# A last chunk of 512 tokens, keys copied in halves, 64 by 64 quarters of the array for eight pairs of heads, and a new list order

## The chip, the cores and the metric

The kernel runs on one core of one Trainium2 chip. The metric is device time in microseconds of one execution; the time before is the median of 3 runs, 616.33 us (616.15 to 616.97). The engines are TensorE (matmuls and transposes, PE in the rows; its weight loads have a row of their own, PEld), VectorE (DVE), ScalarE (ACT), GpSimd (POOL), and SyncE (SP), which issues the DMAs. Each engine works through its own instructions in the order in which the program gives them, and waits at an instruction until its inputs are there and its output may be overwritten.

## The reference

For q, k, v of 2 batches, 8 heads, 768 positions and 64 channels, each query sees the 31 keys less than 16 positions away and 24 block keys, each the maximum over 32 positions of k; the values of the blocks are means of v. Scores are scaled by 1/8, block scores get log(32) added, and a softmax runs over both kinds together. The heads are put side by side to 1536 tokens of 512 channels. Two feed-forward layers of width 2048 follow:

```
x = attention(q, k, v)                                 # 1536 x 512
h = max(x @ w_in1, 0);  x = (h * h) @ w_out1
h = x @ w_in2
g = (a0 + a1 h + a2 h^2 + a3 h^3) / (1 + |b0| |h| + |b1| h^2 + 1e-6)
out = g @ w_out2
```

## The kernel before

**The feed-forward layers.** Each factor is split into a high and a low part (xh and xl, wh and wl, sh and sl), and a product is three matmuls: high by high, high by low, low by high. A layer's 16 slices of 128 hidden channels are split over two passes, 5 and 11 for the first layer (passes 0 and 1), 9 and 7 for the second. A pass goes over chunks of tokens; pass 0 has six of 256 tokens (`tok1`, line 543), the later passes three of 512 (`tok2`). A step is one slice for one chunk: `l1` (line 555) makes its hidden values in four parts of three matmuls each, `elem_1` and `elem_2` the square of the ReLU, `elem_4` and `elem_5` the split, and `l2` (line 641) adds the slice's share to the chunk's output in four parts of three matmuls. The output of a chunk lies in PSUM banks y0 to y3 (two of them for 256 tokens) until its last slice, then it is copied to SBUF (`acc`).

**The attention.** Work is done in 24 duos: two heads with 256 queries each; duos 0 to 3 are the 8 heads at the first 256 tokens, and so on, so that chunk c of pass 0 needs the duos 4c to 4c + 3. The queries of a duo form four windows of 64; a window's keys are 96 positions and 24 blocks, 120 columns. A duo goes through: `d_t` (two transposes of q), `d_z` (copy to SBUF; each head to its own half of the depth, the other half zeros, two copies on ScalarE), `d_s` (scores: a matmul of 128 x 128 by 120 columns for each window, the 128 rows being the two heads' 64 channels), `d_m` (mask and maximum, VectorE), `d_e` (exponential, ScalarE), `d_r` (sum and reciprocal, VectorE), `d_n` (scaling, GpSimd), `d_p` (four transposes), `d_b` (copy to SBUF, ScalarE or VectorE), `d_o` (eight products with the values), `d_x` and `d_y` (the split into xh and xl, ScalarE and VectorE). The matmuls of fp32 operands, as in `d_s` and `d_o`, show two instructions each in the trace.

The keys are loaded for two heads at a time (`e_load`), put into another order by GpSimd (`k_rel`, line 297, one copy a pair), transposed (`k_tr`), and copied into windows (`k_lin`, two halves). `k_put` adds the block maxima. Block sums of v come from `s_add` and `v_sum`, and `v_put` copies them.

**The order.** Pass 0 and the attention are interleaved by a list written out in the program, `ORDER` (line 19): each entry is a letter for a function and a number, and a star puts its copy on VectorE. The letters of the table at line 719 are: E, Q, q_, J loads of k and q; v, Z, N loads of v; I, T, D, W, M load, three conversion steps and the low half of a weight (DMA, ScalarE, VectorE, ScalarE, GpSimd); P the key copy, t, l, k, c, B the rest for the keys; S, V, u, w block sums of v; q, z, s, m, e, r, n, p, b, o, x, y the stages of a duo; h part of an `l1` (four to a step), i, j, G, H the elementwise work of a step, Y a part of an `l2`. Each engine gets its instructions in the order of this list. What follows the list, from the end of pass 0 on, is laid out by `main_loop`, in which TensorE goes from step to step. PSUM banks for the attention come from a small pool (`bank`, `free`), first in first out.

Of the kernel before, what the change touches and what calls it, by code (L numbers as in the profile page):

```python
# [59 lines left out]
def tile_window_attention_moe_moe(  # L60
# [27 lines left out]
    NWIN = S // LO  # L88
    SC = math.sqrt(D)
    NEG = -1e9 * SC  # L90
    NSLOT, NMORE = 10, 3

    const = ctx.enter_context(tc.tile_pool(name="const", bufs=1))
    wp = ctx.enter_context(tc.tile_pool(name="wp", bufs=NSLOT))
# [763 lines left out]
```

## Time and profile before

| | |
|---|---|
| median of 3 runs | 616.33 us |
| the profiled execution: its own time | 617.99 us |
| its span, first to last instruction | 616.3 us |
| TensorE matmuls busy | 597.6 us, 97% |
| TensorE weight loads busy | 514.0 us, 83% |
| VectorE busy | 390.8 us, 63% |
| ScalarE busy | 402.1 us, 65% |
| GpSimd busy | 345.9 us, 56% |
| granted TensorE clock, mean | 0.999 of full speed |
| first matmul of pass 0 (h0) | 33.18 us |

Busy time of matmuls is the union of overlapping records, so it doesn't say how many fit in. Idle time of an engine counts only where TensorE then waits for it. The mean duration in a group of instructions is that of one instruction from start to end; the time that one more of it takes is the distance between starts in a packed row. A list of waits names what came last before the waiting instruction could start.

### The profile page before, as it was taken

The page shows a single profiled execution, that of the slowest core. Times are in us where ns is not written, and L with a number is a line of the kernel's source. Part 1 is how long each engine was busy: PE and PEld are TensorE (multiplying, and loading weights), DVE is VectorE, ACT ScalarE, POOL GpSimd, SP SyncE. Part 2 cuts the span into 40 slices and gives each one's busy share as a digit, 9 for nine tenths or more (in the row PEclk, how much of TensorE's full clock was granted, in tenths as well). Part 3 has the DMA queues.
Part 4 walks back from the last instruction along what each step waited for, and adds up shares of the span by engine and source line. Part 5 has one row for each costly group of instructions (what it writes and reads, how often), then busy time and mean ns, then how long its engine had stood idle before and what let it go on. Part 6 is the DMA issues. An engine that isn't in the chain of part 4 may idle for free.

```text
span 616.3 us, 9787 instructions
## 1 busy us (share of the span) xinstructions
PE 597.6 (97%) x3488; PEld 514.0 (83%) x3488; DVE 390.8 (63%) x815; ACT 402.1 (65%) x766; POOL 345.9 (56%) x363
## 2 busy tenths in 40 slices
PE   5899998999999999999999999999999999999997
PEld 4789898999988888888888888888888888888885
DVE  5998777666553332111256487898878887686775
ACT  5887566766554443222356598988888887777772
POOL 4777858355664445222557568675656664454442
PEclk9999999999999999999999999999999999999999
DMA  9999894440342331000045202121202200010011
GB/s 220 247 225 213 208 233 96 120 108 16 114 160 72 99 103 35 0 1 0 1 137 179 96 1 69 34 70 34 69 35 69 69 1 0 1 69 1 22 47 68
DMA packets 64145, 51.48 MB, mean 84 GB/s; under 512 B 39777, under 2 KB 56161, under 8 KB 64097
## 3 DMA queue, kind: packets, MB, share of 16 engines
q1 hardware_dynamic: 64096, 50.87, 30.8%
q8 instruction: 27, 0.44, 0.3%
q14 instruction: 22, 0.17, 0.1%
HBM read 47.71 MB, written 3.15 MB: 83 GB/s over the span
## 4 chain that ended last, share of the span: by engine, by line
PE 80%; DVE 1%; ACT 0%; POOL 0%; issue 0%; DVEq 0%; ACTq 0%
PE h L567 39%; PE y L661 38%; PE pss L452 1%; PE pav L517 1%; PE ptp L501 1%; DVE acc L687 0%; PE pt L433 0%; DVE h L616 0%; DVE q L613 0%; ACT h L609 0%; POOL wl L175 0%; DVE p L619 0%; ACT q L588 0%; DVE p L602 0%; DVE pp L505 0%
## 5 line engine op out<-in xcount | busy, mean ns | idle before, releaser
L567 PE MATMUL h<-xh,wh 128*128 128x512 f32 (+1 forms) x444 | 161.9, 365 | 0.0
L567 PE MATMUL h<-xh,wl 128*128 128x512 f32 (+1 forms) x444 | 160.1, 361 | 0.0
L567 PE MATMUL h<-xl,wh 128*128 128x512 f32 (+1 forms) x444 | 160.0, 360 | 0.0
L637 POOL TENSOR_TENSOR sl<-r,sh 128x512 fp32r<-128x512 f32 (+1 forms) x63 | 66.4, 1054 | 119.8 <-PE y L661 76.6
L591 POOL TENSOR_TENSOR q<-q,u 128x512 f32<-128x512 f32 x48 | 63.8, 1330 | 94.7 <-ACT q L588 91.0
L582 DVE TENSOR_TENSOR r<-r,h 128x512 f32<-128x512 f32 (+1 forms) x63 | 35.0, 555 | 113.1 <-ACT r L577 105.6
L567 PEld LDWEIGHTS h<-xh,wh 128*128 128x128 f32 x444 | 83.8, 189 | 12.8
L567 PEld LDWEIGHTS h<-xh,wl 128*128 128x128 f32 x444 | 83.7, 189 | 12.9
L567 PEld LDWEIGHTS h<-xl,wh 128*128 128x128 f32 x444 | 83.8, 189 | 12.4
L175 POOL TENSOR_TENSOR wl<-wdec,wh 128x512 fp32r<-128x512 f32 x64 | 83.3, 1309 | 12.5 <-ACT wh L170 10.5
L661 PE MATMUL y<-sl,wh 128*128 128x512 f32 (+1 forms) x252 | 85.7, 340 | 1.3 <-POOL sl L637 1.3
L661 PE MATMUL y<-sh,wh 128*128 128x512 f32 (+1 forms) x252 | 86.7, 344 | 0.0
L661 PE MATMUL y<-sh,wl 128*128 128x512 f32 (+1 forms) x252 | 85.2, 338 | 0.0
L577 ACT ACTIVATE r<-h 128x512 f32<-128x512 f32 (+1 forms) x63 | 31.1, 494 | 82.5 <-PE h L567 44.1
L661 PE MATMUL y<-wh,sl 128*128 128x512 f32 x192 | 74.8, 390 | 0.1
L661 PE MATMUL y<-wl,sh 128*128 128x512 f32 x192 | 74.7, 389 | 0.0
L661 PE MATMUL y<-wh,sh 128*128 128x512 f32 x192 | 74.7, 389 | 0.0
L637 POOL TENSOR_TENSOR sl<-p,sh 128x512 fp32r<-128x512 f32 x48 | 64.5, 1344 | 9.9 <-ACT sh L630 8.6
L613 DVE SCALAR_TENSOR_TENSOR q<-q,h 128x512 f32<-128x512 f32 x48 | 32.9, 685 | 39.4 <-ACT h L609 39.4
L159 DVE SCALAR_TENSOR_TENSOR wdec<-wraw,wdec 128x512 int32<-128x512 int32 x64 | 56.0, 875 | 2.2
L170 ACT CAST wh<-wdec 128x512 fp32r<-128x512 f32 x64 | 39.7, 621 | 22.6 <-DVE wdec L159 22.5
L661 PEld LDWEIGHTS y<-sl,wh 128*128 128x128 f32 x252 | 47.6, 189 | 6.9 <-POOL sl L637 1.5
(88 smaller groups left out, 1071.8 us busy)
## 6 DMA issues: line engine op xcount, KB each, us to landing
wraw<-in_moe_w_in_dram SPq DMA_DIRECT2D x32, 512.0 KB, 3.9
wraw<-in_moe_w_out_dram SPq DMA_DIRECT2D x32, 512.0 KB, 3.4
early<-in_v_dram SPq DMA_DIRECT2D x40, 96.0 KB, 4.4
out_dram<-acc SPq DMA_DIRECT2D x12, 256.0 KB, 2.1
acc<-in_q_dram SPq DMA_DIRECT2D x10, 256.0 KB, 5.4
early<-in_k_dram SPq DMA_DIRECT2D x4, 384.0 KB, 5.3
early<-in_v_dram SPq DMA_DIRECT2D x4, 384.0 KB, 8.0
kst<-in_k_dram SPq DMA_DIRECT2D x8, 192.0 KB, 7.1
```

The source lines that it names most:

```text
L159: nc.vector.scalar_tensor_tensor(out=t, in0=low, scalar=29, in1=t, op0=ALU.logical_shift_right, op1=ALU.bitwise_or)
L170: nc.scalar.copy(out=wt[n][0][:, j], in_=f32(wdec[n, j]))
L175: nc.gpsimd.tensor_tensor(out=tl[:, j], in0=t, in1=f32(th[:, j]), op=ALU.subtract)
L452: nc.tensor.matmul(pt[:, c * HK:(c + 1) * HK], lhsT=qz[d % 2][:, c].rearrange("p e t -> p (e t)"), rhs=kt[p][:, 2 * i + c], start=c == 0, ...
L501: nc.tensor.transpose(out=pt[0:HK, c * P:(c + 1) * P], in_=pr[:, c, 0:HK], identity=ident)
L567: nc.tensor.matmul(hq[g][:, 0:n], lhsT=w[:, 0, ws], rhs=x[:, part, ts], start=(part == 0 and j == 0), stop=(part == KC - 1 and j == 2),)
L577: nc.scalar.activation(out=r, in_=hq[g][:, 0:n], func=AF.Relu)
L582: nc.vector.tensor_tensor(out=eq[g], in0=eq[g], in1=hq.pop(g)[:, 0:n], op=ALU.mult)
L591: nc.gpsimd.tensor_tensor(out=q_, in0=q_, in1=u_, op=ALU.mult)
L613: nc.vector.scalar_tensor_tensor(out=q_, in0=q_, scalar=1.0 + 1e-6, in1=z_, op0=ALU.add, op1=ALU.mult)
L637: nc.gpsimd.tensor_tensor(out=sl[:, 0:n], in0=eq.pop(g), in1=f32(sh[:, 0:n]), op=ALU.subtract)
L661: nc.tensor.matmul(o, lhsT=lt, rhs=rt, start=(f == 0 and j == 0 and d * m % 512 == 0), stop=(f == FS[ps] - 1 and j == 2 and (d + 1) * m % ...
```

## The change

The last 512 tokens of pass 0 become one chunk of 512 (`tok1`), so that pass 0 has five chunks and 25 steps instead of six and 30; `h` ends at 99 instead of 119 and `Y` in the list at 91 instead of 111. `k_rel` copies half of a pair's positions, P the first and R the second, on GpSimd or, with a star, on VectorE. For the duos 0 to 7 `d_z` is one copy of both heads without zeros, on ScalarE or with a star on VectorE, and `d_s` makes eight matmuls, each head of a window in its own 64 rows and 64 columns of the array, both heads into the same bank. Small tiles get fixed buffers (two of each, as before). The list has another order throughout; its first ten lines (to Y7) and the part about the last duos are shown.

```diff
@@ the list, to Y7, before and after @@
-    "E0 E1 _id P0 _m0 t0 l0 P1 E2 q_0 _z0 t1 q0 k0 _pr k1 I0 P2 q_1 _ml t2 _m1 E3 q1 l1 z0 c0 T0 "
-    "P3 s0 _m2 l2 _bw z1 c1 q2 v0 Q1 S0 D0 v1 m0 k2 B1 s1 e0 z2 t3 I1 c2 m1 v2 r0 e1 l3 s2 k3 v3 "
-    "q3 z3 n0 q4 N0 B2* B0* r1 c3 q5 p0 N1 n1 p1 z4 W0 s3 S1 B3* S2 b0* V0 S3 m2 b1 T1 I2 m3 s4 "
-    "e2 z5 N2 D1 u0* r2 e3 m4 n2 w0* q6 W1 M0 r3 e4 z6 r4 N3 q7 s5 V1 o0 I3 n3 u1 I4 p2 o1 m5 x0 "
-    "w1 b2* y0 s6 T2 p3 o2 D2 b3* e5 n4 x1 r5 x2 y1 h0 M1 z7 o3 p4 W2 x3 y2 O0 Q2 m6 h1 h2 y3 s7 "
-    "M2 b4* n5 N5 h3 N4 T3 I5 D3 h4 e6 T4 h5 h6 I6 h7 D4 q8 i0 W3 p5 j0 J1 z8 J2 W4 M3 m7 q9 M4 "
-    "s8 i1 o4 b5* r6 o5 G0 z9 h8 H0 I7 x4 T5 m8 D5 e7 Y0 Y1 Y2 x5 q10 h9 n6 r7 Y3 T6 h10 J3 D6 "
-    "z10 h11 J0 n7 W5 i2 p6 y4 b6* s9 y5 s10 j1 W6 q11 m9 I8 p7 e8 M6 M5 h12 N7 N6 G1 h13 j2 z11 "
-    "T7 H1 h14 h15 i3 t4 Y4 I9 N8 G2 k4 Y5 b7* T8 r8 D7 W7 H2 Y6 n8 Y7 t5 Y8 Y9 D8 Y10 k5 W8 Y11 "
+    "_pr E0 R0* P0* _id t0 _z0 E3 E1 q_0 _bw _m0 P1* k0 R1 l0 E2 t1 I0 k1 c0 q0 l1* q1 P2 B0 q_1 "
+    "z0 _m1 R2 c1 B1 s0 R3 T0 v1 t2 z1 _ml P3 _m2 q2 k2 l2 v0 Q1 m0 t3 v3 v2 I1 z2 D0 c2 e0 q3 r0 "
+    "l3 s1 k3 s2 m1 S1 m2 e1 S0 V0 n0 r1 q4 c3 n1 S3 z3 N0 W0 B3* q6 e2 S2 p0 q7 p1 z4 u0 w0 b1 "
+    "s3 N1 s4 r2 b0* M0 q5 m3 I2 m4 V1 e3 o0 r3 n2 e4 B2* z6* T1 o1 N2 u1 z5 s5 n3 D1 r4 x0 n4 N3 "
+    "w1 x1 I3 y0 p2 p3 h0 T2 m5 b2 b3 z7* W1 s6 D2 y1 e5 o3 m6 M1 I4 o2 W2 r5 h1 s7 Q2 x2 x3 N4 "
+    "T3 I5 e6 M2 y2 h2 y3 h3 h4 D3 N5 h5 I6 n5 h6 p4 T4 W3 J0 i0 h7 O0 D4 q8 m7 j0 M3 q9 W4 M4 "
+    "b4* z8 J1 p5 i1 r6 b5* G0 q10 e7 s8 h8 z9 h9 T5 H0 Y0 Y1 Y2 m8 r7 Y3 h10 z10 n6 o5 o4 x5 D5 "
+    "n7 p6 y5 T6 W5 x4 D6 s9 h11 b6 I7 t4 W6 M5 M6 y4 l4 i2 m9 k4 j1 s10 q11 p7 G1 h12 I8 j2 T7 "
+    "N6 b7* h13 H1 Y4 Y5 D7 e8 T8 N7 D8 h14 h15 Y6 i3 G2 W7 Y7 o6 W8 H2 r8 o7 M8 Y8 Y9 x7 Y10 I9 "
...
@@ the list after, from s20 to the first Y of the merged chunk @@
+    "p17 n18 z21 q22 s20 i18 b17* G17 h77 m20 o16 z22 r19 H17 o17 s21 e20 n19 N18 p18 m21 x16 Y68 "
+    "Y69 Y70 N19 y16 q23 h78 e21 z23 h79 r20 x17 p19 j18 s23 n20 i19 y17 b19 p20 G18 s22 b18 H18 "
+    "r21 Y71 m23 Y72 n21 m22 o18 o19 p21 Y73 e23 N21 N20 e22 b20 Y74 r23 r22 b21* x19 x18 j19 y18 "
+    "Y75 o20 N22 n23 n22 N23 T19 y19 o21 x20 p23 I21 p22 b23 y20 b22* h80 x21 y21 o23 o22 W18 D19 "
+    "M18 x22 I22 x23 y22 h81 W19 h82 y23 h83 i20 h84 h85 G19 j20 H19 h86 Y76 Y77 M19 T20 Y78 Y79 "
+    "h87 h88 i21 D20 j21 h89 h90 G20 H20 h91 T21 Y80 Y81 Y82 i22 G21 Y83 H21 Y84 W20 Y85 D21 Y86 "
...
@@ -89,6 +86,7 @@
     SC = math.sqrt(D)
     NEG = -1e9 * SC
     NSLOT, NMORE = 10, 3
+    NQUAD = 8
 
     const = ctx.enter_context(tc.tile_pool(name="const", bufs=1))
     wp = ctx.enter_context(tc.tile_pool(name="wp", bufs=NSLOT))
@@ -185,6 +183,10 @@
     KP = VP + 2 * KE
     bw = ap.tile([VP, HK], F32, name="bw", bufs=1)
     qz = [ap.tile([P, 4, 2, LO], F32, name=f"qz{j}", bufs=1) for j in range(2)]
+    qp = [ap.tile([P, 4, LO], F32, name=f"qp{j}", bufs=1) for j in range(2)]
+    pps = [ap.tile([HK, 4, 2, LO], F32, name=f"pp{j}", bufs=1) for j in range(2)]
+    mxs = [ap.tile([P, 8], F32, name=f"mx{j}", bufs=1) for j in range(2)]
+    rss = [ap.tile([P, 4], F32, name=f"rs{j}", bufs=1) for j in range(2)]
     kss = [ap.tile([P, NB], F32, name=f"kss{j}", bufs=1) for j in range(NP)]
     kt = [ap.tile([P, NWIN, HK], F32, name=f"kt{j}", bufs=1) for j in range(NP)]
     NPR = 3
@@ -203,6 +205,7 @@
     kst = const.tile([P, TR, 4, D], F32, tag="xh2", name="kst")[0:VP]
     vst = const.tile([P, 4, TR, D], F32, tag="xl2", name="vst")[0:VP]
     ksrc = {}
+    krel = {}
     vsrc = {}
     banks = ["y0", "y1", "y2", "y3", "a0", "a1"]
 
@@ -294,11 +297,12 @@
         )
         ksrc[p] = t
 
-    def k_rel(p, copy):
+    def k_rel(p, b, copy):
 
         t = early[4 + p][0:VP].rearrange("p (r h d) -> p r h d", r=TR, d=D)
-        copy(out=t.rearrange("p r h d -> p h r d"), in_=ksrc[p])
-        ksrc[p] = t
+        rs = slice(b * TR // 2, (b + 1) * TR // 2)
+        copy(out=t[:, rs].rearrange("p r h d -> p h r d"), in_=ksrc[p][:, :, rs])
+        krel[p] = t
 
     def k_load(h):
 
@@ -359,7 +363,7 @@
 
     def k_tr(p):
 
-        src = ksrc[p].rearrange("p r h d -> p r (h d)")
+        src = (krel if p < NP else ksrc)[p].rearrange("p r h d -> p r (h d)")
         pk[p] = [bank("pk"), bank("pk")]
         for pt in pk[p]:
             nc.vector.memset(pt[:, 0:5 * KP].rearrange("p (r c) -> p r c", c=KP)[:, :, 0:2 * KE], 0.0)
@@ -432,10 +436,13 @@
         for r in range(2):
             nc.tensor.transpose(out=pt[:, r * P:(r + 1) * P], in_=src[:, r], identity=ident)
 
-    def d_z(d):
-
+    def d_z(d, copy=nc.scalar.copy):
 
         pt = pq.pop(d)
+        if d < NQUAD:
+            copy(out=qp[d % 2], in_=pt[:, 0:2 * P].rearrange("p (c t) -> p c t", t=LO))
+            free(pt)
+            return
         for e in range(2):
             r = slice(e * D, (e + 1) * D)
             nc.scalar.copy(
@@ -448,6 +455,15 @@
 
         bb, i, p, _ = at(2 * d)
         pt = psc[d] = bank("pss")
+        if d < NQUAD:
+            for c in range(4):
+                for e in range(2):
+                    r = slice(e * D, (e + 1) * D)
+                    nc.tensor.matmul(
+                        pt[r, c * HK:(c + 1) * HK], lhsT=qp[d % 2][r, c], rhs=kt[p][r, 2 * i + c],
+                        start=c == 0, stop=c == 3,
+                    )
+            return
         for c in range(4):
             nc.tensor.matmul(
                 pt[:, c * HK:(c + 1) * HK],
@@ -459,7 +475,7 @@
 
         i = at(2 * d)[1]
         pt = psc.pop(d)
-        mx = ap.tile([P, 8], F32, tag="mx", name="mx", bufs=2)
+        mx = mxs[d % 2]
         pr = prs[d % NPR]
         pm[d] = mx, pr
         m = 0 if i == 0 else 2 if i == NQ - 2 else 1
@@ -480,7 +496,7 @@
 
     def d_r(d):
         mx, pr = ex.pop(d)
-        rs = ap.tile([P, 4], F32, tag="rs", name="rs", bufs=2)
+        rs = rss[d % 2]
         nc.vector.tensor_reduce(out=mx[:, 4:8], in_=pr, axis=AX.X, op=ALU.add)
         nc.vector.reciprocal(out=rs, in_=mx[:, 4:8])
         pn[d] = rs, pr
@@ -501,7 +517,7 @@
             nc.tensor.transpose(out=pt[0:HK, c * P:(c + 1) * P], in_=pr[:, c, 0:HK], identity=ident)
 
     def d_b(d, copy=nc.scalar.copy):
-        pp = ap.tile([HK, 4, 2, LO], F32, tag="pp", name="pp", bufs=2)
+        pp = pps[d % 2]
         copy(out=pp.rearrange("p c e t -> p (c e t)"), in_=po[d][0:HK])
         free(po[d])
         po[d] = pp
@@ -540,7 +556,7 @@
 
     FS = [5, NF - 5, 9, NF - 9]
     N0 = [0, 5, NF, NF + 9]
-    tok1 = [(G * c, G) for c in range(NT // G)]
+    tok1 = [(G * c, G) for c in range(NT // G - 2)] + [(NT - 2 * G, 2 * G)]
     tok2 = [(2 * G * c, 2 * G) for c in range(NT // (2 * G))]
     passes = [tok1, tok2, tok2, tok2]
     steps = [(ps, c, f) for ps in range(4) for c in range(len(passes[ps])) for f in range(FS[ps])]
@@ -720,7 +736,8 @@
         E=e_load, v=lambda p: s_load(0, 2 * p, v0[p]), Q=q_load,
         N=lambda i: v_load(i // 4, i % 4 // 2, i % 2), J=k_load,
         Z=lambda i: s_load(1, 4 * i, vst), I=lambda i: w_next(3),
-        P=lambda p: k_rel(p, nc.gpsimd.tensor_copy), t=k_tr,
+        P=lambda p, c=nc.gpsimd.tensor_copy: k_rel(p, 0, c),
+        R=lambda p, c=nc.gpsimd.tensor_copy: k_rel(p, 1, c), t=k_tr,
         l=lambda p, c=act: k_lin(p, 0, c), k=lambda p, c=act: k_lin(p, 1, c),
         c=lambda p: k_put(p, some, dve), B=lambda p, c=act: k_put(p, rest, c, False),
         S=lambda p: s_add(v0[p], LEFT) if p < NP else s_add(vst), V=v_sum,
```

## Rows read from the trace of the kernel before

**Rows 1.** Windows of the span: length, busy us by engine, clock, DMA.

```profile
0.00:7.80 7.80, 2.06 (x11) 1.77 (x12) 1.80 (x15) 2.56 (x3) 3.05 (x11) 1.00 0.83 189
7.80:52.50 44.70, 39.55 (x375) 35.73 (x373) 42.19 (x156) 38.58 (x101) 31.93 (x53) 1.00 1.06 236
52.50:110.00 57.50, 53.85 (x564) 52.03 (x562) 41.40 (x128) 36.90 (x97) 40.07 (x63) 1.00 0.79 177
110.00:168.00 58.00, 57.67 (x579) 56.66 (x576) 37.51 (x129) 39.95 (x109) 30.64 (x54) 1.00 0.34 92
168.00:607.00 439.00, 439.00 (x1951) 363.74 (x1949) 264.69 (x385) 283.48 (x457) 238.78 (x184) 1.00 0.16 52
```

**Rows 2.** Waits of TensorE from 0 to 170 us: total us, times, longest.

```profile
PE pk L368 <- POOL early L300: 6.3, 3, 5.6
...
PE y L661 <- POOL sl L637: 1.3, 1, 1.3
```

**Rows 3.** Chain of waits in order of time: start, us, piece.

```profile
110.52 2.86 PE h L567 x24
...
179.61 2.72 PE y L661 x12
```

**Rows 4.** Timeline of the start: start, us, engine, instruction, idle time before it.

```profile
4.49 1.03 POOL L300 COPY early<-early 96x1024 f32<-96x1024 f32 x1 [3.05 <-DMA early<-in_k_dram]
...
6.19 1.04 POOL L300 COPY early<-early 96x1024 f32<-96x1024 f32 x1 [0.67 <-DMA early<-in_k_dram]
...
7.59 1.04 POOL L300 COPY early<-early 96x1024 f32<-96x1024 f32 x1 [0.36 <-DMA early<-in_k_dram]
...
7.83 0.95 DVE L388 TENSOR_REDUCE kss<-kt 128x24 f32<-128x768 f32 x1 [0.52 <-ACT kt L380]
```

**Rows 5.** Groups of instructions by form, whole run: busy us, mean ns of one.

```profile
L159 DVE SCALAR_TENSOR_TENSOR wdec<-wraw,wdec 128x512 int32<-128x512 int32 x64 | 56.0, 875 | 2.2
...
L491 POOL TENSOR_SCALAR pr<-pr,rs 128x120 f32<-128x120 f32 x96 | 35.8, 393 | 5.7 <-DVE rs L485 5.7
...
L158 DVE TENSOR_SCALAR wdec<-wdec 128x512 int32<-128x512 int32 x64 | 33.7, 526 | 10.8 <-ACT wdec L150 7.2 <-issue 3.5
...
L476 ACT ACTIVATE pr<-pr,mx 128x120 f32<-128x120 f32 x96 | 29.7, 385 | 3.6 <-DVE mx L467 3.5
...
L467 DVE CUSTOM_DVE_ANT_0 pr<-pss,mask 128x120 f32<-128x120 f32 x96 | 21.2, 278 | 8.2 <-PE pss L452 6.4 <-PE ptp L501 1.3 <-DVE rs L485 0.2
...
L441 ACT COPY qz<-pt 64x256 f32<-64x256 f32 x48 | 17.5, 365 | 1.5 <-PE pss L452 0.7
...
L484 DVE TENSOR_REDUCE mx<-pr 128x4 f32<-128x484 f32 x24 | 15.6, 652 | 2.2 <-ACT pr L476 1.8
...
L505 DVE COPY pp<-ptp 120x512 f32<-120x512 f32 x17 | 11.5, 684 | 5.4 <-PE ptp L501 3.0 <-PE pav L517 2.2 <-issue 0.2
...
L536 DVE TENSOR_TENSOR xl<-pav,xh 128x256 fp32r<-128x256 f32 x24 | 9.6, 418 | 3.5 <-ACT xh L531 3.3
...
L485 DVE RECIPROCAL rs<-mx 128x4 f32<-128x4 f32 x24 | 4.3, 178 | 1.8 <-DVE mx L484 0.5
...
L505 ACT COPY pp<-ptp 120x512 f32<-120x512 f32 x7 | 4.1, 581 | 1.8 <-PE pav L517 1.2 <-PE ptp L501 0.5
...
L415 DVE COPY early<-pvs 24x256 f32<-24x256 f32 x10 | 3.9, 425 | 0.2
...
L415 ACT COPY early<-pvs 24x256 f32<-24x256 f32 x6 | 1.9, 363 | 0.1
```

**Rows 6.** Timeline of TensorE around one s and a pair of o.

```profile
96.08 1.04 PE L452 MATMUL pss<-kt,qz 128*128 128x120 f32 x8
96.89 0.36 PE L661 MATMUL y<-sh,wh 128*128 128x256 f32 x1
...
108.96 1.19 PE L517 MATMUL pav<-pp,early 120*64 120x64 f32 x32
110.08 0.44 PE L433 MATMUL pt<-ident,acc 128*128 128x128 f32 x2
```

45 rows, old and new, of the table ORDER are left out of this document.

## The prediction

> **What bounds the kernel now.** I read the windows first, cut where the character of the work changes [rows 1]: the reader compares TensorE's busy time with the length of each window. From 168 to 607 us it is busy 439.00 of 439.00 us: a packed row of matmuls that the change leaves as it is. All that can move lies before 168 us and in the handover. There TensorE idles 5.74 us before 7.8 us, 5.15 us from 7.8 to 52.5 us, and 3.65 us from 52.5 to 110 us. In the second of these windows VectorE is busy 42.19 of 44.70 us and ScalarE 38.58: TensorE waits there because VectorE, and nearly ScalarE, are full. Next the waits of TensorE [rows 2]: 6.3 us are for GpSimd's copy of the first keys, the rest single waits of about 1 us for VectorE, ScalarE or GpSimd at many lines. No single wait is worth more than 1.3 us after the first key. So the change can win in three places only: fewer microseconds of matmul, a VectorE that is less full before 52 us, and odd waits.
>
> How matmuls are counted matters more than anything else here. Matmuls overlap, so the duration of a single one doesn't say what one more of it costs. The chain of waits shows the spacing [rows 3]: 24 of 256 columns in 2.86 us, 119.2 ns each; 12 of 512 columns in 2.72 us, 226.7 ns each. Two short ones thus cost only 12 ns more than the long one that replaces them.
>
> **The change, part by part.**
>
> *One chunk of 512.* Pass 0 has six chunks of five steps of 24 matmuls of 256 columns. Chunks 4 and 5 become one: 240 matmuls of 119.2 ns are replaced by 120 of 226.7 ns. 28.6 - 27.2 = **1.4 us less** TensorE work. The elementwise work of these steps halves in number and grows in size; it lies beside TensorE, after 110 us, where VectorE and ScalarE are busy under 70% [rows 1], so I count nothing.
>
> Its price: chunk 4 could run beside the attention of the last four duos (20 to 23), and chunk 5 after it. The new chunk needs all eight duos 16 to 23, so after h79 and Y75 the list has no matmul left that doesn't depend on them. I follow the end by hand. From the end of s22 TensorE still has Y71 to Y75 (5 x 0.36), o18 to o21 (4 x 0.56, half of a pair of duos [rows 6]), p21, p23, p22 (0.4 each, an estimate: four transposes of 128 columns at the 0.1 us of an instruction of s), h80 and h81 (0.68 each) and o23 (0.56): 7.2 us. The chain that it must cover is duo 22, behind duo 23 on each engine: m22 0.88, e22 1.24 behind part of e23 (another 0.5), r22 0.83, n22 1.49 behind part of n23 (0.6), p22 0.4, b22 0.68, o22 0.56, x22 and y22 0.42 each (x taken like y), all from [rows 5, 6]: 8.0 us, with o22 on TensorE itself. So 8.0 - 7.2 = **0.8 us** of new idle time before h82. Bounds: nothing (o22 counted as cover, 7.7 against 8.0), and 5 us if the engines' queues are some 4 us late there.
>
> *Keys in halves, P0, R0 and P1 on VectorE.* Before, GpSimd's copy of a pair starts at 4.49 us and takes 1.03, and TensorE waits for it 5.6 us long [rows 2, 4]. No row shows this copy on VectorE; a half has 512 elements a partition, and the nearest is the 120x512 copy at 0.684 us [rows 5], which reads the other memory. Two of them would end no earlier than GpSimd's (1.37 against 1.03); at half that price 0.35 us earlier. I take nothing, bounds -0.4 and +0.4.  The new list loads E3 (384 KB) ahead of E1: pair 1 lands where pair 2 landed, whose copy began at 7.59, not 6.19 [rows 4]. P1 on VectorE waits there, and the first block maxima (c0, at 7.83 in the trace) stand behind it on VectorE: about **0.5 us late**, which goes into the next item. The three halves on VectorE run while it waits for keys.
>
> *The order up to Y7, and one copy for q.* Up to Y7 both lists give TensorE the very same work (5 t, 12 q, 11 s, 2 V, 8 p, 6 o, 16 h, 7 Y), so what the other two engines have in front of it can be set against each other. VectorE, old to new: r 9 to 8 (-0.83), copies b 7 to 4 (-2.05), u and w 2 to none (four copies of 0.425, -1.70), D 8 to 9 (+1.40), and z6 and z7 as one 128x256 copy each (+0.84, by the 0.418 of the nearest form); one B fewer and one l more I let cancel: **-2.3 us** [rows 5]. ScalarE: 12 z of two copies of 0.365 become 6 single ones (at 0.365 too) and 3 of two, -4.4; three b more +1.74, u and w +1.45: **-1.2 us** [rows 5]. VectorE was the fuller; its 2.3 less the 0.5 of the late start leave 1.8, and ScalarE lets through only 1.2 where it is the later one. I take **1.4 us** less idle time before 52 us, between the two; bounds 0 (both then wait for each other) and 2.3.
>
> *An own quarter of the array for each head, duos 0 to 7.* Four matmuls of depth 128, half of it zeros, become eight of 64 by 64. In instructions, 8 become 16. Before, the next matmul begins 0.81 us after s does: 0.101 us each; the nearest row of a 64-wide kind is o, 32 in 1.12 us, 0.035 each at 64 columns [rows 6]. The new ones stream 120. By o's price 16 cost 0.56; by s's, side by side in pairs, 0.81; one after another 1.62. I take 0.81, so **nothing**; bounds for eight duos -2.0 and +6.5 us. The row of o shows two column halves following each other at 35 ns into one bank; it doesn't show two row halves. The Trainium skill, TensorEngine Tiling (Array Packing), Restrictions and Gotchas, says that different row tiles cannot access the same PSUM bank at the same time, and both heads of a duo write one bank here. By that rule the third rival below; no run shown here bears it out yet.
>
> *Odd waits after 52 us.* Of the 3.65 us the largest is 1.3 us for GpSimd's low half [rows 2]. VectorE enters this stretch 2 us less behind, so waits for it should shrink, while others appear elsewhere: **-0.5 us**, bounds -3 and +2.
>
> Sum: -1.4 + 0.8 + 0 - 1.4 + 0 - 0.5 = **-2.5 us**. The profiled execution took 617.99 us, 1.69 of it outside its span of 616.3; it would be 615.5. It lies 1.66 above the median of 616.33, and that part isn't in the kernel's span, so the median becomes **613.8 us**. Less than 0.2% (1.2 us) can't be told from no change.
>
> **Rivals.**
> 1. *More odd waits go.* Only a few 1 us waits follow from a want of throughput: after 110 us every engine but TensorE has 30% in hand. If 1.8 of the 3.65 us go, VectorE's relief of 2.3 us is felt less the 0.5 and the end costs 0.3: -1.4 - 1.8 - 1.8 + 0.3 = -4.7, 611.6 us. Against it: a list in fixed order makes as many single waits as it removes.
> 2. *No change.* ScalarE, relieved by 1.2 only, takes VectorE's place (it was at 38.58 of 44.70 us and now copies more of VectorE's tiles), so 0.4 comes of the early part, and the end costs 1.4: -1.4 - 0.4 + 1.4 = -0.4, 615.9 us.
> 3. *Slower: the two heads' quarters don't run side by side.* Then s of duos 0 to 7 costs 1.62 instead of 0.81, 6.5 us in all, in the 40 us in which 5.15 - 1.4 = 3.8 us of idle time is left; half of that, 1.9, may hide it: 613.8 + 4.6 = 618.4 us. It decides from about 3.7 us of it left open, 0.24 us a duo more than is hidden. For it: the instruction count doubles. Against it: o's 35 ns.
> 4. *Slower: the last duos are late.* GpSimd one duo and one low half behind at s22 (1.49 + 0.77) and ScalarE a T or W of 0.6 to 0.7 give 3 to 4 us more idle time before h80 to h83: 617.5 us or so. It decides from 3.7 us. Against: GpSimd is busy 30.64 of the 58 us [rows 1].
>
> **How the numbers follow.** Forecast 0.45 (its own range 612.0 to 615.1), rival 1 0.13, rival 2 0.22, rival 3 0.11, rival 4 0.09. Faster: 0.45 x 0.93 + 0.13 + 0.22 x 0.1 = 0.57; within 0.2%: 0.03 + 0.20 + 0.01 = 0.24; slower 0.19. The range runs from 610.4 (rival 1 with another 1.2 us) to 618.2, which leaves most of rival 3 out and keeps rival 4 in.
>
> **What would show it.** Twenty-four merged matmuls still 5.44 us apart and those of 256 columns at 119 ns; TensorE's idle time from 7.8 to 52 us at 3.5 to 4; s of duos 0 to 7 followed by the next matmul after about 0.81 us (1.6 is rival 3); no wait over 1 us before h80 to h83 (more is rival 4); VectorE still the fuller engine before 52 us (if ScalarE, rival 2). The prediction fails if the start of pass 1 doesn't come 2 to 3 us earlier than before, or if TensorE no longer runs without a gap from there.

## The result, and the profile after

The changed kernel takes **610.77 us** (610.16 to 611.24, 5 runs) beside 616.33 of the kernel before; the ratio is 0.9901 [0.9880, 0.9922], 5.56 us less. The forecast was 613.8: the sign is right and the time lies in the range, but more than twice the forecast gain came, and most of it from a term that was put at 0.5 us. The prediction had named 2 to 3 us for the start of pass 1; it comes 9.62 us earlier, or 7.04 without the 2.58 us by which the matmuls behind that mark have grown (below).

The windows of the profile after, cut as in [rows 1] (the start of pass 1 now at 158.7), with the same columns: length, then busy us of TensorE, its weight loads, VectorE, ScalarE, GpSimd, then clock and DMA.

```profile
0.00:7.80 7.80, 1.51 (x8) 1.25 (x8) 2.74 (x15) 2.18 (x3) 1.42 (x11) 1.00 0.84 195
7.80:52.50 44.70, 42.36 (x440) 37.80 (x440) 40.36 (x155) 36.75 (x99) 32.66 (x52) 1.00 1.02 237
52.50:110.00 57.50, 57.50 (x605) 56.53 (x604) 45.83 (x143) 43.89 (x116) 44.03 (x68) 1.00 0.89 191
110.00:158.70 48.70, 48.70 (x416) 43.81 (x415) 30.39 (x105) 33.49 (x86) 27.04 (x47) 1.00 0.36 93
158.70:600.30 441.60, 441.55 (x1948) 365.42 (x1947) 262.44 (x385) 282.99 (x456) 239.07 (x184) 1.00 0.17 52
```

From 52.5 us to the end of the attention TensorE doesn't idle at all; before it idled 3.65 us there [rows 1]. From 7.8 to 52.5 us 2.34 us of idle time are left instead of 5.15. The waits of TensorE from 0 to 170 us (us in total, times, longest) fall together to three lines, all before 52 us; those of [rows 2] are gone:

```profile
PE pk L372 <- DVE pk L369: 7.4, 4, 5.4
PE pss L462 <- ACT qp L443: 0.6, 2, 0.4
PE pss L468 <- ACT qz L448: 0.5, 1, 0.5
```

Where the time went is seen best by two marks that mean the same work in both kernels: the start of the last matmul of Y7 and of the first of pass 1. First the kernel before, then the changed one (timeline of TensorE):

```profile
52.49 0.28 PE L661 MATMUL y<-sl,wh 128*128 128x256 f32 x1
...
168.34 0.40 PE L567 MATMUL h<-xh,wh 128*128 128x512 f32 x1
```

```profile
52.37 0.28 PE L677 MATMUL y<-sl,wh 128*128 128x256 f32 x1
...
158.72 0.39 PE L583 MATMUL h<-xh,wh 128*128 128x512 f32 x1
```

Y7 ends at the same time in these two executions (in a_tight, a_split and h_newold below, which are the same up to there, the mark lies at 51.57, 52.53 and 53.83 us, so a difference of 1 us there says little). Between the marks lie 115.85 us before and 106.35 after, 9.50 less. Of these 2.58 aren't won: 24 matmuls of the last `l2` stand behind the second mark in both kernels, of 512 columns now (24 x 0.2267 us against 24 x 0.1192). The merge takes 1.43 (as forecast, by the spacings). **5.49 us are left, in the stretch for which the forecast had 0.5**: 3.98 of idle time (115.80 us with 111.82 busy against 106.20 with 106.20, windows from 52.5 us to the start of pass 1), the rest in busy time; a part of that are the last matmuls before each wait, which count as busy for their whole record (last section). From pass 1 to the end nothing moved: 443.78 us from the second mark to the start of the last matmul (612.12) before, and 446.22 (to 604.94) after with the 2.58 in it.

The profiled executions differ by 7.18 us (617.99 and 610.81), the medians by 5.56: the profiled run of before was 1.66 over its median, that of after 0.04. So some 1.6 of the 5.49 likely belong to that one execution, and some 3.8 to the change. For comparison, b_quad below, the kernel before with the quarters and its list unmoved, has 114.97 us between the marks in its profiled execution, 2.72 of them idle.

### The profile page after: what moved, and what is told of

Same layout as the page of the kernel before. It is cut to its first block, busy times and chain, and to the rows that moved or that the text cites. A ratio compares the mean times of both kernels' runs of the same rounds, so it can differ in the third digit from the quotient of the medians.

```text
span 609.1 us, 9652 instructions
## 1 busy us (share of the span) xinstructions
PE 596.7 (98%) x3432; PEld 508.6 (84%) x3432; DVE 384.5 (63%) x803; ACT 399.9 (66%) x758; POOL 345.5 (57%) x359
## 4 chain that ended last, share of the span: by engine, by line
PE 93%; ACT 3%; DVE 2%; DMA 1%; issue 0%; SPq 0%; DVEq 0%; ACTq 0%
PE h L583 43%; PE y L677 42%; PE pss L468 2%; PE pav L533 2%; PE ptp L517 2%; PE pk L372 1%; DMA early<-in_k_dram 1%; ACT pr L492 1%; PE pss L462 1%; PE pt L437 1%; PE pvs L411 0%; DVE acc L703 0%; ACT wdec L148 0%; DVE kt L398 0%; DVE h L632 0%
## 5 line engine op out<-in xcount | busy, mean ns | idle before, releaser
L583 PE MATMUL h<-xh,wh 128*128 128x512 f32 (+1 forms) x424 | 158.5, 374 | 0.0
L583 PE MATMUL h<-xl,wh 128*128 128x512 f32 (+1 forms) x424 | 156.6, 369 | 0.0
L583 PE MATMUL h<-xh,wl 128*128 128x512 f32 (+1 forms) x424 | 156.5, 369 | 0.0
L583 PEld LDWEIGHTS h<-xh,wh 128*128 128x128 f32 x424 | 79.9, 188 | 13.6 <-issue 0.2
L583 PEld LDWEIGHTS h<-xl,wh 128*128 128x128 f32 x424 | 79.9, 188 | 13.5 <-DVE xl L552 0.2
L583 PEld LDWEIGHTS h<-xh,wl 128*128 128x128 f32 x424 | 79.9, 188 | 13.3
L677 PE MATMUL y<-sh,wh 128*128 128x512 f32 (+1 forms) x232 | 83.2, 359 | 0.0
L677 PE MATMUL y<-sl,wh 128*128 128x512 f32 (+1 forms) x232 | 81.9, 353 | 0.0
L677 PE MATMUL y<-sh,wl 128*128 128x512 f32 (+1 forms) x232 | 81.8, 352 | 0.0
L603 ACT ACTIVATE u<-h 128x512 f32<-128x512 f32 x48 | 28.6, 595 | 31.4 <-PE h L583 31.3
```

Of the source, the lines that this page charges most:

```text
L583: nc.tensor.matmul(hq[g][:, 0:n], lhsT=w[:, 0, ws], rhs=x[:, part, ts], start=(part == 0 and j == 0), stop=(part == KC - 1 and j == 2),)
L603: nc.scalar.activation(out=u_, in_=hq[g][:, 0:n], func=AF.Abs)
L677: nc.tensor.matmul(o, lhsT=lt, rhs=rt, start=(f == 0 and j == 0 and d * m % 512 == 0), stop=(f == FS[ps] - 1 and j == 2 and (d + 1) * m % ...
```

## Experiments

Each ratio is to the kernel before, on the same chip, with a 95% interval. "Between the marks" is Y7 to pass 1 of the profiled execution, as above.

**Waits of the old list, one by one.** In the old list I moved what its three largest waits behind 52 us came from: the DMA of block values that GpSimd's adds ahead of a low half wait for, a weight conversion ahead of a copy on ScalarE, both, and both with o8 to o15 some entries later.

```diff
-  ... j12 l7 Y47 c6 D14 s13 Z1 m12 ...      # Z1 now directly behind V2 (b_vst_early, b_both, b_fix)
-  ... S4 b8* N10 G6 T11 h33 ... p9 j7 I12 b9 h35 ...   # T11 now directly behind b9 (b_w_late, b_both, b_fix)
-  p14 s16 I17 W14 r15 o12 n15 N15 b14* u3 w3* x12 o13 y12 p15 h60 b15* o14 x13 o15 ...   # b_fix, and two like it
+  I17 W14 r15 o12 o13 x12 x13 p14 y12 n15 N15 b14* s16 u3 w3* y13 p15 h60 b15* q17 T15 h61 o14 o15 ...
```

> The kernel before, with one entry of the list moved: Z1, the load of the second batch's v for the block sums (768 KB), stands right after V2, the last reader of its tile, and not 62 entries later. Theory A (a late DMA makes single waits): in the trace of before GpSimd stands 2.77 us at 93.2 us waiting for this load, then adds for 4.74 us, and the low half H12 behind it comes 1.31 us late for TensorE; the 0.86 us wait at 107 us follows from the same delay. With the load some 2 to 3 us earlier both shrink: 1.3 to 2.2 us faster than before, about 614.5. Theory B (a list in fixed order keeps its number of single waits, the forecast's reason for only 0.5 us): another wait takes their place, 616.3 within 0.5.

> The kernel before, with one entry moved: T11, ScalarE's first conversion step of a weight, stands after b9 and not eleven entries ahead of it. Theory A: in the trace of before ScalarE stands 1.49 us at 69.4 us waiting for that weight's DMA, with e11 and the copy b9 behind it, for which TensorE waits 1.24 us at 71.7 us; without it 1.2 us faster, about 615.1. Theory B: another wait takes its place, 616.3 within 0.5.

> Both moves in the kernel before. Theory A: they add up, 2.5 to 3.5 us faster than before, about 613.3, with at most 1 us of TensorE's 3.65 us of idle time between 52.5 and 110 us left. Theory B: 616.3 within 0.7, the idle time of that window still about 3.6 us at other lines.

> The kernel before with both moves (Z1 early, T11 late) and, in three places of the list (duos 8 and 9, 10 and 11, 12 to 15), the products o put one to three entries of TensorE later, so that TensorE has 0.7 to 1.8 us of other work between the transposes p and the products o that need their copy b. Theory L (the waits after 52 us are handovers placed too tightly in the list): the idle time of TensorE between 52.5 and 110 us falls below 0.7 us and the end comes 2 to 4 us earlier, about 613.3. Rival: the waits move on to the next handover, idle time 2 us or more and 616.

Measured: 617.57 us, 1.0018 [1.0007, 1.0028]; 616.34, 0.9996 [0.9983, 1.0009]; 616.75, 1.0003 [0.9991, 1.0015]; 618.11, 1.0023 [1.0011, 1.0035]. Nothing is won; the first and the last are 0.2% slower. The waits of TensorE in b_both behind 52.5 us (the largest three of six):

```profile
PE pav L517 <- DVE pp L505: 1.2, 2, 0.9
PE y L661 <- ACT sh L630: 0.5, 1, 0.5
PE y L661 <- POOL sl L637: 0.3, 1, 0.3
...
```

The 1.3 us of [rows 2] for the low half are 0.3 here, and a wait for its high half, on ScalarE, stands beside it. But b_quad, in which no entry was moved, has the same two:

```profile
96.90 0.39 PE L676 MATMUL y<-sh,wh 128*128 128x256 f32 x1 [0.46 <-ACT sh L645]
...
97.71 0.39 PE L676 MATMUL y<-sl,wh 128*128 128x256 f32 x1 [0.31 <-POOL sl L652]
```

So the 1.3 us may belong to the one profiled execution of before, and that a moved entry made one wait into another isn't shown. TensorE's idle time between the marks is 2.62 us in b_both and 2.11 in b_fix beside b_quad's 2.72, and no median falls.

**The merge apart.** The changed kernel with chunks 4 and 5 of 256 tokens; its list is kept up to h83.

```diff
-    tok1 = [(G * c, G) for c in range(NT // G - 2)] + [(NT - 2 * G, 2 * G)]
+    tok1 = [(G * c, G) for c in range(NT // G)]
```

> The changed kernel with its last chunk cut into two of 256 tokens again (six chunks, 30 steps), its list otherwise kept up to h83; both short chunks stand where the merged one stood. Theory A: the merging is worth the spacing alone, 120 x 12 ns = 1.4 us, so 612.2. Rival: the merging is worth more than that, for instance by halving the number of elementwise steps and of banks handed over; then 613.5 or more.

612.55 us, 0.9934 [0.9920, 0.9949], between the marks 110.73, and no idle time from 52.5 to 110 us. The merge is worth 1.8 us (612.55 - 610.77) where the spacings say 1.4; the other 3.8 come without it.

**The start.** Identity matmuls ahead of t0 and t1 (a_warm), more of them and also ahead of s0 and t2 (a_warm2), pair 1 of the keys loaded ahead of pair 3 (a_swap), the three copies of halves on GpSimd (a_gpkeys).

```diff
-  ... R0* P0* _id t0 _z0 E3 E1 ... P1* k0 ... E2 t1 ...
+  ... R0* P0* _id _w8 t0 _z0 E3 E1 ... P1* k0 ... E2 _w3 t1 ...   # a_warm; a_warm2 also _w2 s0, _w6 t2
+  ... R0* P0* _id t0 _z0 E1 E3 ...                                # a_swap
+  ... R0 P0 _id t0 _z0 E3 E1 ... P1 k0 ...                        # a_gpkeys
```

> The changed kernel with eleven matmuls of the identity by itself added on TensorE, eight ahead of t0 and three ahead of t1, into a bank that nothing reads; they stand where TensorE waits for keys. In the trace of the changed kernel eight transposes of t take 1.5 us until 17 us (0.85 later), two transposes of q 0.63 (0.38 later), and s of duos 0 to 2 about 1.8 us (0.96 from duo 4 on), while the kernel before was at its fast durations from 11 us. Theory W: TensorE runs slower there for want of work before, and its own chain from 15.5 to 26 us sets the pace; kept busy from 1.5 us on it is fast at once, t3, q and s1, s2 cost 2.6 us less, and the end comes 1.5 to 2.6 us earlier: about 608.7. Rival: VectorE and ScalarE set the pace of the first 50 us, 610.8 within 0.5.

> The changed kernel with nineteen matmuls of the identity on TensorE: eight ahead of t0, three ahead of t1, two ahead of s0 and six ahead of t2, so that the 1.6 us gap at 12.5 us is filled too, behind which the granted clock fell to 0.50 in the run with eleven. Theory W: now TensorE stays at its fast durations, s1 and s2 take 0.96 us and not 1.7, and the end comes 1 to 2.5 us earlier, about 609. Rival: VectorE and ScalarE set the pace of the first 50 us, 610.8 within 0.5.

> The changed kernel with E1 and E3 exchanged in the list, so that the second pair of keys is loaded second and the fourth third. Theory: the second pair lands 1.2 to 1.4 us earlier, and as the chain of waits of the changed kernel begins with that load (1.7 to 7.5 us), 0.5 to 1.2 us faster, about 609.9. Rival: VectorE and ScalarE are behind anyway, 610.8 within 0.4.

> The changed kernel with all key halves copied by GpSimd, none by VectorE. In the changed kernel VectorE copies the first pair in 0.76 us, GpSimd needs 0.86 for one half, so t0 starts 1 us later, and behind it the first scores. Theory: VectorE's part in the keys is worth 0.5 to 1.2 us, 611.8. Rival: nothing, since VectorE then is free earlier for the maxima: 610.8 within 0.4.

611.14 us, 0.9919 [0.9897, 0.9941]; 610.73, 0.9925 [0.9895, 0.9954]; 610.83, 0.9908 [0.9889, 0.9927]; 611.17, 0.9914 [0.9899, 0.9928]: none can be told from the changed kernel. The timeline of TensorE shows what stands against each other, first the changed kernel, then a_warm2 (start, us, instruction, idle time before it):

```profile
13.43 1.51 PE L372 MATMUL pk<-ident,early 96*128 96x96 f32 x8 [0.69 <-DVE pk L369]
...
15.55 1.51 PE L372 MATMUL pk<-ident,early 96*128 96x96 f32 x8 [0.18 <-DVE pk L369]
...
17.42 3.66 PE L462 MATMUL pss<-kt,qp 64*64 64x120 f32 x32
21.01 2.01 PE L411 MATMUL pvs<-early,bw 96*120 96x128 f32 x16
```

```profile
13.18 0.85 PE L386 MATMUL pk<-ident,early 96*128 96x96 f32 x8 [0.51 <-DVE pk L383]
...
15.31 0.85 PE L386 MATMUL pk<-ident,early 96*128 96x96 f32 x8 [1.05 <-DVE pk L383]
16.00 0.39 PE L451 MATMUL pt<-ident,acc 128*128 128x128 f32 x2
16.31 1.04 PE L476 MATMUL pss<-kt,qp 64*64 64x120 f32 x16
18.91 1.04 PE L476 MATMUL pss<-kt,qp 64*64 64x120 f32 x16 [1.56 <-DVE kt L412]
19.88 2.01 PE L425 MATMUL pvs<-early,bw 96*120 96x128 f32 x16
```

With the identity matmuls the transposes take 0.85 instead of 1.51 us and the two s 2.0 instead of 3.66, but now TensorE waits 1.05 and 1.56 us for VectorE's part of the keys: 1.1 us are won at the values (19.88 against 21.01), and the median doesn't show them.

**The quarters.** No quarters in the new list (a_noquad); the two heads one after the other instead of in turn (a_heads); quarters and single copy in the old list (b_quad).

```diff
-    NQUAD = 8
+    NQUAD = 0                            # a_noquad; b_quad: the lines of NQUAD put into the kernel before
-            for c in range(4):
-                for e in range(2):
+            for e in range(2):           # a_heads
+                for c in range(4):
```

> The changed kernel without the quarters of the array: d_z and d_s of duos 0 to 7 as before (two copies with zeros between, four matmuls of 128 by 128), the list kept. Theory S: ScalarE's chain sets the pace from 26 to 40 us in the changed kernel, eight second copies of 0.365 us give it 2.9 us more there: 1 to 2.5 us slower, about 612.5. Rival: they are hidden, and s falls from 0.96 to 0.81 us a duo: 610.8 or up to 1 us faster.

> The changed kernel with the eight matmuls of d_s in another order in duos 0 to 7: all four windows of the one head, then all four of the other, and not head by head in turn. Theory P: neighbours in different quarters run side by side, so s rises from 0.96 us a duo towards twice that and the kernel gets 1 to 4 us slower, 612 to 615. Rival: they follow one another anyway, 610.8 within 0.4, and s keeps its 0.96 us.

> The kernel before with the quarters of the array for duos 0 to 7 alone (one copy z on ScalarE, eight matmuls s), the list as it was. Without them the changed kernel lost 3.3 us. Theory S: the relief of ScalarE by 2.9 us helps the old list as well, 1 to 3 us faster than before, about 614.3. Rival: the gain needs the new list, whose first 50 us lean on it; the old list, in which VectorE is the fuller engine there, gains less than 0.7 us, 615.9.

a_noquad: 614.04 us, 0.9966 [0.9951, 0.9981], 3.3 more than the changed kernel. Its windows (columns as above) and the first of its waits up to 52.5 us:

```profile
7.80:52.50 44.70, 39.80 (x353) 36.52 (x354) 37.82 (x148) 38.43 (x103) 31.99 (x51) 1.00 0.95 222
52.50:110.00 57.50, 57.40 (x600) 56.17 (x600) 46.27 (x143) 43.79 (x118) 42.77 (x66) 1.00 0.89 193
```

```profile
PE pss L468 <- ACT qz L448: 3.0, 3, 1.4
```

The loss is nearly all ahead of Y7 (its last matmul starts at 55.34), for the larger part in waits for ScalarE's two copies a duo; between the marks it takes 106.88 us, with 0.1 us idle. So the quarters don't make the row without gaps; it is the single copy that comes with them that ScalarE needs to follow the new list up to Y7. b_quad: 617.38, 1.0016 [1.0000, 1.0031], Y7 at 52.38: in the old list they bring nothing.

a_heads: 615.19 (611.34 to 617.05), 0.9969 [0.9951, 0.9988]. The timelines, first of a_heads, then of the changed kernel, show one s and what follows it:

```profile
31.43 1.50 PE L462 MATMUL pss<-kt,qp 64*64 64x120 f32 x16 [0.31 <-ACT qp L443]
32.85 1.09 PE L517 MATMUL ptp<-ident,pr 128*120 128x128 f32 x8
```

```profile
30.15 1.04 PE L462 MATMUL pss<-kt,qp 64*64 64x120 f32 x16 [0.17 <-ACT qp L443]
31.12 1.09 PE L517 MATMUL ptp<-ident,pr 128*120 128x128 f32 x8
```

In turn 16 instructions take 0.97 us, 61 ns each, head by head 1.42, 89 ns each: neighbours in different quarters overlap more than neighbours in the same one, though both write one bank. Whether it is the matmuls themselves or the weight load of one with the matmul of the other, these rows don't separate. The Trainium skill, TensorEngine Tiling (Array Packing), Restrictions and Gotchas, says that different row tiles cannot access one PSUM bank simultaneously; if that meant any two row tiles in one bank, I would expect little gain from taking turns, and the 0.45 us here speak against that reading; no row shows the writes themselves.

**The two lists crossed.** Up to Y7 both lists hold the same matmuls, so they can be joined there. h_newold: the parts of a_split, new list up to Y7, old order behind. h_oldnew: the changed kernel with the old order up to Y7, the new one behind; h_oldnew_nq the same without quarters.

```diff
+  # h_newold:  "_pr E0 R0* P0* _id t0 ... Y6 i3 G2 W7 Y7" + "r8 ... t5 Y8 Y9 Y10 k5 W8 Y11 o6 ... T23 M22 D23 W23 M23" (old)
+  # h_oldnew:  "E0 E1 _id P0 R0 _m0 t0 ... H2 Y6 n8 Y7" (old) + "l4 D8 o6 W8 o7 M8 Y8 ... W22 Y91 W23 M22 M23"
```

> All parts of the change but the merge (the last two chunks of pass 0 stay apart); the list is the new one up to Y7, and behind it every entry in the order of the list before. Up to Y7 both lists give TensorE the same work. From Y7 to the first matmul of pass 1 the profiled execution took 115.85 us before and 110.73 with the new list throughout and the chunks apart. Theory A (the order behind Y7 takes the waits away): 115 to 116 us again, TensorE idle 3 to 4 us between 52.5 and 110 us, median near 616. Theory B (the order up to Y7, with the quarters, leaves VectorE and ScalarE less work behind, and the waits go by that): 110.7 to 111.5 us, idle under 1 us, median near 612.5.

> The changed kernel (merge, quarters, halves of keys), its list in the order of before up to Y7 (each R directly behind its P, both on GpSimd), and in the new order behind it. With the merge the new list throughout took 106.35 us from Y7 to the first matmul of pass 1. Theory A (the order behind Y7): about 106.4 to 107 us, hardly any idle time behind 52.5 us, median 610.5 to 611.5. Theory B (what the order up to Y7 leaves behind): only the merge remains, 114 us, median near 614.5.

> As the kernel with the old order up to Y7 and the new one behind it, but duos 0 to 7 with zero-padded q and the whole array again. Theory A (the order behind Y7 takes the waits away, and the quarters were only wanted because the new list is tighter for ScalarE up to Y7): Y7 near 52.5 us as before, hardly any idle time behind it, median 610.5 to 611.5, no more than 0.5 above its neighbour with quarters. If the quarters are worth their 3.3 us in this list too: 614.

h_newold: 618.25 us, 1.0017 [0.9995, 1.0039], between the marks 116.56. h_oldnew: 612.89, 0.9937 [0.9914, 0.9960], 108.73. h_oldnew_nq: 612.85, 0.9927 [0.9902, 0.9952]. All waits of TensorE behind 90 us in h_newold but the last one (timeline):

```profile
97.08 0.44 PE L440 MATMUL pt<-ident,acc 128*128 128x128 f32 x2 [0.44 <-DVE mx L486]
99.94 0.39 PE L680 MATMUL y<-sh,wh 128*128 128x256 f32 x1 [0.46 <-ACT sh L649]
100.75 0.38 PE L680 MATMUL y<-sl,wh 128*128 128x256 f32 x1 [0.31 <-POOL sl L656]
109.21 0.69 PE L536 MATMUL pav<-pp,early 120*64 120x64 f32 x16 [0.86 <-DVE pp L524]
110.11 0.63 PE L520 MATMUL ptp<-ident,pr 128*120 128x128 f32 x4 [0.21 <-DVE early L422]
```

b_both has the same five at the same distances, 3.84 or 3.85 us earlier, and four of them as long to a hundredth:

```profile
93.24 0.44 PE L433 MATMUL pt<-ident,acc 128*128 128x128 f32 x2 [0.25 <-DVE mx L467]
96.09 0.39 PE L661 MATMUL y<-sh,wh 128*128 128x256 f32 x1 [0.46 <-ACT sh L630]
96.90 0.39 PE L661 MATMUL y<-sl,wh 128*128 128x256 f32 x1 [0.30 <-POOL sl L637]
105.37 0.69 PE L517 MATMUL pav<-pp,early 120*64 120x64 f32 x16 [0.86 <-DVE pp L505]
106.27 0.62 PE L501 MATMUL ptp<-ident,pr 128*120 128x128 f32 x4 [0.21 <-DVE early L415]
```

They belong to the old order, whatever ran ahead of it; b_quad has them too. Ahead of 90 us h_newold has two more: 0.34 us at 73.39 and, at its join, one for a load of keys (J2 and J3 stand ahead of Y7 in the old list and directly behind it here):

```profile
55.64 0.85 PE L375 MATMUL pk<-ident,kst 96*128 96x96 f32 x8 [1.53 <-DMA kst<-in_k_dram]
```

So 1.53 us of what h_newold loses against a_split, 5.8 between the marks, are the price of this join and not of the order behind it. And h_oldnew has only two waits behind Y7 (same view), both within 12 us of the join:

```profile
53.59 1.24 PE L533 MATMUL pav<-pp,early 120*64 120x64 f32 x32 [1.25 <-ACT kt L384]
...
63.80 0.39 PE L677 MATMUL y<-sh,wl 128*128 128x256 f32 x1 [0.74 <-POOL wl L173]
```

**The join.** What is left between 612.9 and 610.8 may be the join: l4 stood ahead of o6. It is moved up behind k4, with quarters (h_seam) and without (h_seam_nq).

```diff
-  ... k4 Y5 b7* ... n8 Y7 l4 D8 o6 W8 ...
+  ... k4 l4 Y5 b7* ... n8 Y7 D8 o6 W8 ...
```

> As h_oldnew (merge, quarters, old order up to Y7, new order behind it), with l4 moved directly behind k4: in h_oldnew it stood between Y7 and o6, and TensorE waited 1.25 us before o6 until this copy of keys had ended and another 0.74 us at 63.8 us. If the 2.1 us between h_oldnew and the changed kernel are the join of the two halves, both waits go and the median is 611 to 611.5. If the new order up to Y7 is worth them by itself, it stays at 612.5 to 613.

> As h_seam with zero-padded q and the whole array for duos 0 to 7. If the join was the difference: 610.8 to 611.5, and neither the quarters nor the new order up to Y7 are needed for the gain. If not: 612.5 to 613.5.

613.23 us, 0.9947 [0.9927, 0.9966]; 613.64, 0.9953 [0.9934, 0.9972]. Not settled: o6 now waits for a load of v instead, and the second wait stays (h_seam):

```profile
53.70 1.35 PE L533 MATMUL pav<-pp,early 120*64 120x64 f32 x32 [1.39 <-DMA early<-in_v_dram]
63.99 0.39 PE L677 MATMUL y<-sh,wl 128*128 128x256 f32 x1 [0.71 <-POOL wl L173]
```

The new order behind Y7 takes o6 earlier than the old one had prepared for. Whether another join would win the 2 us without the new order ahead of Y7 stays open.

**Less cover between p and o.** p of duos 9, 10, 11, 18 and 19 just ahead of their copy b (p18 then stands behind m21, which takes over its tile, so that duo 18 uses duo 21's numbers).

```diff
-  j8 p9 H7 ... h38 b9 h39 ... x8 p10 y9 ... q12 b10* ... N10 p11 D12 z12 Y32 b11 ...
+  j8 H7 ... h38 p9 b9 h39 ... x8 y9 ... q12 p10 b10* ... N10 D12 z12 Y32 p11 b11 ...
```

> The changed kernel with p of duos 9, 10, 11, 18 and 19 moved to just ahead of their copy b, so that less TensorE work stands between p and o: 0.4, 1.5, 0.9, 1.2 and 1.9 us or so instead of 2.5, 2.1, 1.3, 5.4 and 3.5. If the waits behind 52.5 us are a matter of this cover, those with less than the 1 us of p's end, the copy (0.61 to 0.68) and its hand-over wait again: 0.5 to 1.5 us idle, median 611.3 to 612.3. If the engines' slack alone keeps the waits away: no idle time, 610.8.

613.14 us, 0.9940 [0.9918, 0.9962], between the marks 108.46 instead of 106.35. Waits of TensorE from 52.5 to 150 us, of which the changed kernel has none:

```profile
PE pss L468 <- ACT qz L448: 0.4, 1, 0.4
PE pav L533 <- DVE pp L521: 0.3, 1, 0.3
PE pav L533 <- ACT pp L521: 0.3, 1, 0.3
```

Five entries moved, of 822, bring three waits back and cost 2.4 us by the median, 2.1 between the marks of the profile, twice the 1.1 that the waits show. Cover is thus part of what the new order gives. That it is all of it isn't shown: its other pairs were not tried.

## Why the prediction was wrong in size

- **One chunk of 512: right.** The chain after has 24 merged matmuls in 5.44 us, as worked out, and the merge apart is worth 1.8 us against 1.4:

```profile
145.28 5.44 PE y L677 x24
```

- **The end of the attention, +0.8: it was 0**, its lower bound. No wait stands before h80 to h83, and rival 4 falls with it: the other engines were not behind. The hand count let the queues of ScalarE and GpSimd delay duo 22 by about half a microsecond each; nothing of it reaches TensorE.
- **Keys in halves, 0: not contradicted.** VectorE's first two halves take 0.76 us together, and the first key transpose starts at 5.36 instead of 5.58 us; with all halves on GpSimd the time is 611.17 us, which can't be told from 610.77. Halves as such were not tried against whole copies.
- **Order up to Y7, -1.4: it was 0 at Y7** (52.37 against 52.49 us). VectorE's work fell by 1.8 us in this window (42.19 to 40.36), ScalarE's too, and VectorE stays the fuller one, the prediction's own sign against rival 2. Yet behind 20 us the two waits that are left (0.17 and 0.53 us) are both for ScalarE's copies, and the 0.1 us at Y7 is nearer to rival 2's 0.4 for this part than to 1.4, so that rival was half right. Idle time from 7.8 to 52.5 us fell by 2.8 us, twice what was forecast, but TensorE's busy time rose by as much. The quarters add 0.16 us a duo to it (0.97 against 0.81), and instructions run at half pace until about 21 us (s1 and s2 3.66 us for 32, later 0.97 for 16), where in the kernel before a pair of q's transposes is at full pace from 11.83 us on:

```profile
10.33 0.64 PE L433 MATMUL pt<-ident,acc 128*128 128x128 f32 x2
...
11.83 0.38 PE L433 MATMUL pt<-ident,acc 128*128 128x128 f32 x2
```

The forecast counted idle time alone and had no term for the pace; the granted clock of these stretches stands in the last section. Yet undoing that (a_warm2) won nothing by the median: VectorE's keys are the next limit right behind it. At Y7 the new list isn't ahead of the old one, and without quarters it is 3 us behind.
- **Quarters, 0 with 0.81 us a duo: 0.97 at full pace.** Rival 3 (1.62) did not come: neighbours do overlap in the order of the kernel, and even head by head the price would have been 1.42. In this list the quarters with their single copy are worth 3.3 us, in the old one nothing: a part can't be priced apart from the order that leans on it.
- **Odd waits behind 52 us, -0.5: the step that failed.** All 3.65 us of idle time went; by the medians what goes beside the merge is 3.8 us, beyond the bound of 3. I had reasoned that a fixed list makes as many single waits as it removes. Patches of the old list indeed win nothing (four kernels, 616.3 to 618.1). A list ordered anew is another matter: of the eight kernels with the whole new order seven show no wait behind Y7 in the list of waits, a_warm2 one of 0.28 us; the joined ones wait at the join, and h_seam and h_seam_nq once more, for a load of v at 138 us (0.29 and 1.51). After 52 us no engine but TensorE is full (VectorE 41.40 of 57.5 us, ScalarE 36.90, [rows 1]), so none of these waits is a want of throughput, and an order can take them all. Rival 1 said just this, took half of it (1.8) and gave 611.6, the nearest of the four; I gave it 0.13. Its nearness is luck in part: it also counted 1.8 us ahead of Y7 that did not come. Of the 3.1 us between forecast and result this term makes 3.3, the end 0.8 and the merge 0.4, and the 1.4 that failed ahead of Y7 take some of that back.
- **The 1.66 us between profiled execution and median** I put outside the kernel's span. Both profiled runs lie 1.7 us above their spans; the 1.66 lay inside, likely in waits. Only differences of medians price the change.

So the 5.6 us are about 1.8 for the merge, 2.1 to 2.7 for the new order behind Y7 (ratios 0.9937 and 0.9927 are 3.9 and 4.5 us, less the merge), and 1 to 2 that need the new order up to Y7 with the quarters, by itself or as what readies the work behind it. Each ratio is uncertain by some 0.2%, 1.2 us, so the split is rough; that the order behind Y7 is needed isn't in doubt, for without it nothing is left of the gain: h_newold is 5.1 us slower than a_split by the two ratios, and the wait at its join explains some 1.5 of that.

## What to carry to other kernels

Where only the bounding engine is full, single waits of a fixed order aren't noise that stays: all of their idle time can go, so bound such a term by the whole of it and not by habit. Moving single entries won nothing here; order the whole stretch anew, with more of the bound engine's work between each producer and consumer. Price a change of order and the parts it leans on together, by crossed halves of the lists if need be.

## What the runs showed of the hardware

TensorE's early instructions took about twice as long as later ones: eight transposes of keys 1.51 us in the changed kernel at 13.43 and 15.55 us, 0.85 in a_warm2 at 13.18 and 15.31, where identity matmuls had filled most of the time from 1.49 us on. This is the granted clock, but the windows don't show it. The trace has records of the granted clock only from some time on, and a window counts the time without a record as 1.00. The first record, at full clock (2.4 GHz), begins at 10.97 us in the kernel before, at 20.93 us in the changed kernel and at 7.14 us in a_warm2, and that is where the durations change: the pair of q's transposes falls from 0.64 to 0.38 us between 10.33 and 11.83 us before, and in the changed kernel 32 instructions of s take 3.66 us from 17.42 us on, 16 later ones 1.04 at 30.15. In a_warm the clock is recorded as full from 10.60 us, at half (1.2 GHz) from 14.01 to 20.84 us, after TensorE had idled since 12.54, and as full from there on; its eight transposes take the same 1.51 us in that stretch as those of the changed kernel ahead of any record. The windows from 15 to 20 us, first of the changed kernel, then of a_warm:

```profile
15.00:20.00 5.00, 4.82 (x36) 3.85 (x36) 4.90 (x15) 3.64 (x9) 2.14 (x2) 1.00 1.20 243
```

```profile
15.00:20.00 5.00, 4.81 (x36) 4.11 (x35) 4.64 (x17) 3.66 (x9) 3.08 (x2) 0.50 1.20 229
```

So the 1.00 in the first two windows, here and in [rows 1], says nothing of the time ahead of the first record, and the new list got its full clock some 8 us later than the old one: the first record lies between 19.63 and 21.97 us in the seven kernels that begin with the new list and have neither identity matmuls nor pair 1 of the keys loaded first, between 10.97 and 14.06 in the ten that begin with the old one. Read the pace from the durations of one kind of instruction, beside the clock.

And a wait costs more than its idle time: in a_tight 1.1 us of waits went with 2.1 us more between the marks. Part of it is that the matmul ahead of a wait counts as busy for its whole record. At the wait of 1.31 us in the kernel before, the matmuls on its two sides start at 97.09 and 98.69 us, 1.60 us apart and not 0.12 as in a packed row, and the next one at 98.91: 1.58 us are lost. Three such waits would make 0.8 of the 1.0 us beyond the idle time of a_tight, an estimate from this one.
